# Attention and gated MLP in float32: VectorE block transposes and v products in eight 32x64 tiles from the fifth pair on

## The chip, the cores and the metric

The kernel runs on one core of one Trainium2 chip. The metric is the device time of one execution in microseconds. A core has TensorE (PE, with its weight loads listed apart as PEld), VectorE (DVE), ScalarE (ACT), GpSimd (POOL), SyncE (SP, which issues the DMAs here) and 16 DMA engines.

## The reference

Batch 8, 8 heads, 576 positions, head width 64, model width 512, all float32. Rotary attention is followed by an MLP with a spatial gate:

```python
q_rot, k_rot = (rotate(q), rotate(k))
scores = scale * np.matmul(q_rot, k_rot.transpose(0, 1, 3, 2))
scores = scores - np.max(scores, axis=-1, keepdims=True)
attn = np.exp(scores)
attn = attn / (np.sum(attn, axis=-1, keepdims=True) + 1e-09)
x = np.matmul(attn, v)                       # heads joined to 512 columns
...
h = np.maximum(x @ w_in, 0.0)
u, v = (h[..., :d_ff // 2], h[..., d_ff // 2:])
v_n = (v - mu) / np.sqrt(var + 1e-06)
v_s = np.einsum('ts,bsd->btd', w_spatial, v_n) + b_spatial[None, :, None]
out = (u * v_s) @ w_out
```

## The kernel before

**Pairs.** Two heads of one batch make a pair: 32 pairs, four to a batch. A pair has nine score tiles of 128 queries by 576 keys: four of head 0, four of head 1, and one that holds the last 64 queries of both heads. For each tile TensorE computes scores (`sc`, L542), VectorE the negated row maximum (`nmx`, L563), ScalarE the exponentials with their row sums (`e`, L565). Exact products of float32 are made of a hi part (rounded to the fp32r format by ScalarE) and a lo part (the rest): `qs` and `ks` hold, stacked over 128 partitions, hi and lo of q against hi of k, and `lk` with `qz` (q of one head, zeros for the other) adds hi of q times lo of k.

**Turning and multiplying.** The v product needs the exponentials with keys on the partitions. In the 28 pairs from the fifth on, `values` (L567) does so in three chunks of three tiles: for each of five key blocks, TensorE turns three 128x128 blocks into PSUM (`tp`, L582), ScalarE takes the hi part out (`eh`, L593), VectorE the lo part (`el`, L312), and TensorE multiplies both with v's hi and lo parts (`vs`) into `pv` (L606). Of `pv`, rows 0 to 63 and 64 to 127 are two partial sums; ScalarE copies one (`avt`, L623) and VectorE adds (`x`, L621). The first four pairs (`PLAIN`) use `values_plain` (L626): the same transposes, plain copies out, and float32 products without a split (L679). A float32 product shows as two records in the trace, a product of fp32r as one.

**Preparing a pair.** `prepare` (L381) loads q and k with their swapped halves (`st`), v (`vr`), applies the rotary table on GpSimd (`tabs` for k, `tabq`, a table already scaled by 1/8, for q), splits, and stacks by ten copying DMAs (`qs`, `ks`, `qz`). v's parts are made on ScalarE and GpSimd (L442, L443).

**MLP.** Per batch, `mlp` runs in four stages of matmuls, `pa`, `pb`, `pc` and `pd` (L750, L773, L791, L806), spread between the attention work of the next batch; the last batch's MLP stands alone at the end.

**Order.** Each operation is recorded with a key (its due time, 20 to a pair), costs by engine, and the buffers that it takes. `Program.run` plays the list through with those costs and emits, on each engine, the ready operation with the lowest key whose buffers are free. So the order on each engine is fixed in the program. `SLOTS` says how many buffers a pool has: PSUM has two score buffers of two banks (`sc`), one bank `pv` and three banks `pm` (for `tp` and the MLP).

Of the kernel before, what the change touches and what calls it, by code (L numbers as in the profile page):

```python
# [16 lines left out]
P = 128  # L17
S = 576
# [12 lines left out]
LATENCY = {PE: 200, ACT: 142, DVE: 118, POOL: 95, DMA: 1700}  # L31
TO_PE = 105
LATE = 1500
SLOTS = {
    "stage": 2, "lk": 1, "vraw": 2, "vs": 2, "e2": 4, "e1": 2, "eh": 7, "rb": 1, "x32": 1, "xg": 7, "m": 4,
    "small": 3, "nmx": 3, "rt": 2, "sc": 2, "pv": 1, "pm": 3,
}
PSUM = {"sc": 1024, "pv": 512, "pm": 512}
# [6 lines left out]
CHUNKS = [  # L45
# [54 lines left out]
class Op:  # L100
    def __init__(self, costs, key, f, new, port):
        self.costs, self.key, self.f, self.new, self.port = costs, key, f, new, port
        self.eng, self.late = None, 0
        self.waits, self.after, self.bufs = 0, [], []


class Program:
# [30 lines left out]
    def run(self, make):  # L138
# [22 lines left out]

        busy = dict.fromkeys(LATENCY, False)
# [5 lines left out]
        while events:  # L168
# [23 lines left out]
            for e in LATENCY:  # L192
# [3 lines left out]
                while ready[e] and not chosen:  # L196
                    item = heapq.heappop(ready[e])
                    if item[2].eng:
                        continue
                    other = {DVE: POOL, POOL: DVE}.get(e)  # L200
                    if item[2].port and other and held[other]:
                        passed.append(item)
                    elif place(item[2].new):
                        chosen = item[2]
                    else:
                        passed.append(item)
                for item in passed:
                    heapq.heappush(ready[e], item)
# [15 lines left out]
def tile_attention_gated_mlp(  # L224
# [47 lines left out]
    tabq = T([P, 2 * S], F32, "tabq")  # L272
    ident = T([P, P], F32, "ident")
# [10 lines left out]
    ks = [T([P, TW + S], F32R, f"ks{a}") for a in range(2)]  # L284
    qz = T([P, 2 * S], F32R, "qz")
# [4 lines left out]
    def setup():  # L290
# [5 lines left out]
        fill(qz[64:P, :S], 0.0)  # L296
        fill(qz[0:64, S:], 0.0)
# [19 lines left out]
    def decode(key, where, at, src):  # L317
# [29 lines left out]
        op(DMA, 1500, key - 8, fetch, w=[t0, t1])  # L347
# [9 lines left out]
    def spatial(key, j):  # L357
        st = Buf("xg", [P, 2, S], F32, f"ws{j}")
        op(DMA, 1700, key - 8, lambda: load(st.tile, w_spT[j * P:(j + 2) * P, :].rearrange("(c p) t -> p c t", p=P)), w=[st], new=[st])
# [20 lines left out]

    def prepare(i):  # L381
# [4 lines left out]
        st = [Buf("stage", [P, 2 * S + TW], F32, f"st{i}_{j}") for j in range(2)]  # L386
        lk = Buf("lk", [P, TW + S], F32R, f"lk{i}")
        vr = Buf("vraw", [P, NQ, 2, D], F32, f"vr{i}")
        vs = Buf("vs", [P, NQ, 2, 2, D], F32R, f"vs{i}")
        prepped.append((lk, vr if i < PLAIN else vs))  # L390

        def hi(j, rows=slice(0, P)):

            return st[j][rows, S:2 * S + TW * j].bitcast(F32R)

        def lo_q(e):
            rest_lo(e, st[0][:, :S].bitcast(F32R), st[0][:, :S], hi(0))
# [19 lines left out]
        op(ACT, 573, key - K_HIQ, lambda: round_hi(hi(0), st[0][:, :S]), r=[(st[0], 0)], w=[(st[0], 1)])  # L417
        pair_op(S, key - K_LOQ, lo_q, r=[(st[0], 1)], w=[(st[0], 0)])

        def hi_k():  # L420
            round_hi(hi(1)[:, TW:], st[1][:, :S])
            round_hi(hi(1)[:, :TW], st[1][:, 4 * P:S])

        def lo_k(e):
            rest_lo(e, lk[:, TW:], st[1][:, :S], hi(1)[:, TW:])
            rest_lo(e, lk[:, :TW], st[1][:, 4 * P:S], hi(1)[:, :TW])

        op(ACT, 720, key - K_HIQ, hi_k, r=[(st[1], 0)], w=[(st[1], 1)])
        pair_op(S + TW, key - K_LOK, lo_k, pieces=2, r=[(st[1], 0), (st[1], 1)], w=[lk], new=[lk])
        for a in range(2):  # L430
# [3 lines left out]
            zd = qz[:, a * S:a * S + S]  # L434
            for dst, rows, j, part, tok in (
                (qd, own, 0, 1, ("qs", a, 0)), (kd, own, 1, 1, ("ks", a, 0)), (kd, oth, 1, 1, ("ks", a, 1)),
                (zd, own, 0, 1, ("qz", a)), (qd, oth, 0, 0, ("qs", a, 1)),
            ):
                op(DMA, 650, key - (K_STACK2 if a else K_STACK), lambda dst=dst, rows=rows, j=j, part=part, own=own: load(dst[rows, :].bitcast(F32), hi(j, own).bitcast(F32) if part else st[j][own, :S]), r=[(st[j], part)], w=[tok])
        if i < PLAIN:  # L440
            return
        op(ACT, 627, key + K_V, lambda: round_hi(vs[:, :, :, 0, :], vr.tile), r=[vr], w=[(vs, 0)], new=[vs])  # L442
        pair_op(2 * NQ * D, key + K_VLO, lambda e: e.tensor_tensor(out=vs[:, :, :, 1, :], in0=vr.tile, in1=vs[:, :, :, 0, :].bitcast(F32), op=ALU.subtract), r=[vr, (vs, 0)], w=[(vs, 1)])  # L443

    def prepare_whole(i, b, hp, key):

        q, k = (Buf("xg", [P, 2 * S], F32, f"st{i}_{j}") for j in range(2))
        kf = Buf("xg", [P, TW + S], F32, f"kf{i}")
        vr = Buf("vraw", [P, NQ, 2, D], F32, f"vr{i}")
        prepped.append(((q, kf), vr))  # L450
# [5 lines left out]
        def sum_k(e):  # L456
            e.tensor_tensor(out=kf[:, TW:], in0=k[:, :S], in1=k[:, S:], op=ALU.add)
            e.tensor_tensor(out=kf[:, :TW], in0=k[:, 4 * P:S], in1=k[:, S + 4 * P:], op=ALU.add)

        if i == 0:  # L460
# [4 lines left out]
            op(ACT, 1053, -50, lambda: nc.scalar.activation(tabq, tabs, AF.Copy, scale=0.125), r=["tabs"], w=["tabq"])  # L465
# [13 lines left out]
        else:
            for j, st in enumerate((q, k)):  # L480
                t = ("tabq", "tabs")[j]
                op(DMA, 1640, key - K_LOAD, lambda j=j, st=st: load(st.tile, qk[b, hp, j].rearrange("p c n -> p (c n)")), w=[(st, 0), (st, 1)], new=[st])
                for part in range(2):
                    pair_op(S, key - K_ROPE, lambda e, st=st, part=part, t=(tabq, tabs)[j]: e.tensor_tensor(out=turn(st, part, slice(0, S)), in0=turn(st, part, slice(0, S)), in1=turn(t, part, slice(0, S)), op=ALU.mult), r=[t], w=[(st, part)])
            pair_op(S, key - K_SUM, lambda e: e.tensor_tensor(out=q[:, :S], in0=q[:, :S], in1=q[:, S:], op=ALU.add), r=[(q, 1)], w=[(q, 0)])
            pair_op(S + TW, key - K_SUM, sum_k, pieces=2, r=[(k, 0), (k, 1)], w=[kf], new=[kf])
        op(DMA, 910, key - K_LOAD + 1, lambda: load(vr.tile, v[b, hp]), w=[vr], new=[vr])


    def attention(i):  # L490
        b, hp = pairs[i]
        lk, vs = prepped[i]
        sm = sums[i % 2]
        x32 = Buf("x32", [P, S], F32, f"x32_{i}")
        todo = []
        for c, (tiles, spans) in enumerate(CHUNKS):
            key = 20 * i + 20 / 3 * c
            e2 = Buf("e2", [P, 2 * S], F32, f"e2_{i}_{c}")
            e1 = Buf("e1", [P, S], F32, f"e1_{i}_{c}")
            for n, (a, t) in enumerate(tiles):  # L500
                scores(i, a, t, lk, sm, key + S_AT[n], e1 if n == 2 else e2, n)
            todo.append((key + K_T, c, spans, e2, e1))
        todo.sort(key=lambda x: x[0])
        for n, (key, c, spans, e2, e1) in enumerate(todo):
            values(i, c, spans, e2, e1, vs, x32, key, None if n == 0 else todo[0][1])
# [443 lines left out]
```

## Time and profile before

| | us |
|---|---|
| median of 3 runs | 966.54 (965.38 to 966.99) |
| span of the profiled execution, first to last instruction | 963.6 |
| DMA, mean over the span | 129 GB/s |

The profiled execution has no time of its own on record beside its span; the median of the runs lies 2.9 us above it. In the profile, busy time is the union of an engine's records. Records of TensorE overlap, since the array is pipelined; how long a product holds the queue is read from one start to the next. The DMA engines' busy share in 40 slices of the span, and what they moved:

```profile
DMA  7775634455354554346444444445524455430101
GB/s 273 240 233 170 191 106 124 130 125 140 103 136 127 159 141 114 102 116 171 124 135 118 117 149 122 127 122 152 149 74 132 123 167 144 110 83 13 62 1 50
```

### The profile page before, as it was taken

Reading aid. Unit: us, or ns where it says so; the run is one execution under the profiler, and the core shown is the slowest. Engines: PE = TensorE matmul, PEld = TensorE weight load, DVE = VectorE, ACT = ScalarE, POOL = GpSimd, SP = SyncE. Lnnn points to the kernel's source line nnn. Section 1 sums busy time; section 2 is a strip of 40 time slices with the busy share of each in tenths; the row PEclk is TensorE's granted clock in tenths of the full one; section 3 lists DMA queues with packets and bytes.
Section 4 is the critical chain, followed back from the end, with each engine's and each line's share of the span. In section 5 each row is a group of like instructions: output and inputs, shape, how many; then the busy total and the mean of one; then the engine's idle time right before and its main releaser. Section 6 shows DMA issues by size and latency. Waiting matters only on the chain.

```text
span 963.6 us, 19472 instructions
## 1 busy us (share of the span) xinstructions
PE 934.0 (97%) x6614; PEld 856.2 (89%) x6614; DVE 656.6 (68%) x1461; ACT 738.2 (77%) x1835; POOL 601.1 (62%) x526
## 2 busy tenths in 40 slices
PE   4988899999999999999999999999999999999998
PEld 2555589999899989999899998999889998999998
DVE  5898686766867677665776658676676766866331
ACT  4887788777987779777897779877798678976452
POOL 6775766576758557774765766666586765672121
PEclk9998999999999999999999999999999999999999
DMA  7775634455354554346444444445524455430101
GB/s 273 240 233 170 191 106 124 130 125 140 103 136 127 159 141 114 102 116 171 124 135 118 117 149 122 127 122 152 149 74 132 123 167 144 110 83 13 62 1 50
DMA packets 56037, 124.64 MB, mean 129 GB/s; under 512 B 13185, under 2 KB 13441, under 8 KB 55938
## 3 DMA queue, kind: packets, MB, share of 16 engines
q1 hardware_dynamic: 55938, 123.40, 46.0%
q8 instruction: 53, 0.87, 0.4%
q14 instruction: 46, 0.38, 0.1%
HBM read 66.03 MB, written 9.58 MB: 78 GB/s over the span
## 4 chain that ended last, share of the span: by engine, by line
PE 75%; ACT 13%; DVE 6%; issue 2%; DMA 2%; POOL 1%; SPq 0%; ACTq 0%; DVEq 0%; POOLq 0%
PE sc L542 13%; PE pc L791 12%; PE pv L606 11%; PE tp L582 11%; PE pd L806 10%; PE pb L773 9%; PE pa L750 5%; ACT e L565 4%; ACT eh L593 2%; DVE nmx L563 2%; ACT vv L837 2%; PE pv L679 1%; PE sc L552 1%; DVE el L312 1%; ACT st L309 1%
## 5 line engine op out<-in xcount | busy, mean ns | idle before, releaser
L593 ACT ACTIVATE eh<-tp 128x384 fp32r<-128x384 f32 (+1 forms) x504 | 217.9, 434 | 85.4 <-PE tp L582 68.2
L312 DVE TENSOR_TENSOR el<-tp,eh 128x384 fp32r<-128x384 f32 x336 | 185.9, 554 | 101.9 <-ACT eh L593 88.0
L563 DVE TENSOR_REDUCE nmx<-sc 128x1 f32<-128x576 f32 x288 | 214.9, 749 | 47.9 <-PE sc L542 40.7
L565 ACT ACTIVATE e<-sc,nmx 128x576 f32<-128x576 f32 x288 | 213.2, 741 | 40.1 <-DVE nmx L563 36.0
L582 PE MATMUL tp<-ident,e 128*128 128x128 f32 (+1 forms) x1176 | 195.6, 273 | 1.3 <-DVE eh L312 0.4
L401 POOL TENSOR_TENSOR st<-st,tabq 128x576 f32<-128x576 f32 x62 | 87.9, 1435 | 134.0 <-DMA st<-in_qk_dram 104.5
L582 PEld LDWEIGHTS tp<-ident,e 128*128 128x128 f32 (+1 forms) x1176 | 145.8, 138 | 16.3 <-issue 3.0
L606 PE MATMUL pv<-eh,vs 128*128 128x384 f32 (+1 forms) x560 | 154.5, 317 | 1.5 <-ACT x L685 1.4
L791 PE MATMUL pc<-wsp,vn 128*128 128x288 f32 x768 | 143.1, 303 | 0.0
L773 PE MATMUL pb<-x,wi 128*128 128x288 f32 x768 | 141.8, 306 | 0.6 <-ACT u L776 0.5
L806 PE MATMUL pd<-g,wo 128*128 128x288 f32 x768 | 141.3, 303 | 0.0
L542 PE MATMUL sc<-ks,qs 128*128 128x288 f32 x620 | 133.1, 304 | 4.8 <-ACT e L565 4.3
L750 PE MATMUL pa<-wi,x 128*128 128x512 f32 x448 | 133.2, 407 | 0.0
L542 PE MATMUL sc<-lk,qz 128*128 128x288 f32 x558 | 120.4, 297 | 0.0
L806 PEld LDWEIGHTS pd<-g,wo 128*128 128x128 f32 x768 | 114.0, 189 | 3.4 <-DVE el L312 0.4
L791 PEld LDWEIGHTS pc<-wsp,vn 128*128 128x128 f32 x768 | 114.6, 189 | 1.8
L773 PEld LDWEIGHTS pb<-x,wi 128*128 128x128 f32 x768 | 112.1, 189 | 4.4 <-PE pb L773 1.1
L542 PEld LDWEIGHTS sc<-ks,qs 128*128 128x128 f32 x620 | 100.8, 190 | 15.9 <-ACT e L565 7.2
L606 PE MATMUL pv<-el,vs 128*64 128x384 f32 (+1 forms) x448 | 113.9, 295 | 0.1
L606 PEld LDWEIGHTS pv<-eh,vs 128*128 128x128 f32 x560 | 97.7, 188 | 7.8 <-DVE x L621 2.0
L716 POOL TENSOR_TENSOR x<-x,rb 128x576 f32<-128x576 f32 x32 | 45.9, 1435 | 79.2 <-DVE x L621 73.1
L312 DVE TENSOR_TENSOR eh<-tp,eh 64x256 fp32r<-64x256 f32 (+1 forms) x168 | 59.8, 356 | 51.8 <-ACT eh L593 28.2
(166 smaller groups left out, 1540.6 us busy)
## 6 DMA issues: line engine op xcount, KB each, us to landing
st<-in_qk_dram SPq DMA_DIRECT2D x64, 576.0 KB
ks<-st SPq DMA_DIRECT2D x124, 160.0 KB
qs<-st SPq DMA_DIRECT2D x124, 144.0 KB
vr<-in_v_dram SPq DMA_DIRECT2D x32, 320.0 KB
qz<-st SPq DMA_DIRECT2D x62, 144.0 KB
out_dram<-ob SPq DMA_DIRECT2D x31, 288.0 KB
ws<-in_w_spT_dram SPq DMA_DIRECT2D x2, 576.0 KB
tabs<-in_tab_dram SPq DMA_DIRECT2D x1, 576.0 KB
```

The costliest lines, as they stand in the source:

```text
L312: eng.tensor_tensor(out=lo, in0=src, in1=hi.bitcast(F32), op=ALU.subtract)
L401: f = lambda e: e.tensor_tensor(out=st[j][:, cols], in0=st[j][:, cols], in1=(tabs if j else tabq)[:, cols], op=ALU.mult)
L542: nc.tensor.matmul(pt[:, c * 512:c * 512 + HALF], lhsT=lhsT, rhs=rhs[:, k0 + c * HALF:k0 + (c + 1) * HALF], start=(n == 0), stop=(n == len ...
L563: op(DVE, 665, key + K_MAX, lambda: nc.vector.tensor_reduce(out=nmx.tile, in_=tops(), op=ALU.max, axis=AX.XY, negate=True), r=[pt], w=[nmx ...
L565: op(ACT, 730, key + K_EXP, lambda: nc.scalar.activation(e[:, e0:e0 + S].rearrange("p (c n) -> p c n", c=2), tops(), AF.Exp, bias=nmx.tile ...
L582: nc.tensor.transpose(out=tp[:e.shape[1], m * P:m * P + P], in_=e, identity=ident)
L593: nc.scalar.activation(h, p, AF.Copy)
L606: nc.tensor.matmul(pv[0:rows, c1:c2], lhsT=vs[:, kt, h, vp, :], rhs=part[:, c1:c2], start=(kt == 0 and n == 0 and c1 == 0), stop=last)
L750: nc.tensor.matmul(pm.tile, lhsT=lhsT, rhs=win[1, d][:, j, :], start=(d == 0 and n == 0), stop=(d == 3 and n == len(todo) - 1))
L773: nc.tensor.matmul(pm[:, :HALF], lhsT=win[0, d][:, i, f * P:(f + 1) * P], rhs=x[d][:, at:at + HALF], start=(d == 0 and n == 0), stop=(d == ...
L791: nc.tensor.matmul(pm[:, :HALF], lhsT=lhsT, rhs=rhs, start=(t == 0 and n == 0), stop=(t == 4 and n == 1))
L806: nc.tensor.matmul(pm[:, :HALF], lhsT=wout[d,][:, i, m * P:(m + 1) * P], rhs=gs[d][:, at:at + HALF], start=(d == 0 and n == 0), stop=(d == ...
```

## The change

From the fifth pair on, TensorE's transposes, the hi and lo parts of the exponentials and the split of v are gone. Each exponentials tile is a slice of one buffer `et` (nine tiles of 576, two such buffers), and VectorE transposes it in place in blocks of 32 by 32 (`turn`). Partition group g (32 partitions) then holds, for key block b, 32 keys of each tile's query group g. So v is loaded four times, once into each group of 32 partitions (`vrep`), and TensorE multiplies in float32: 18 key blocks, in each eight products of 32 rows by 64 columns of weights (four groups, two heads) with 160 or 128 columns moving. The eight write four PSUM banks, one for each group: two of a score buffer (`lower`) and two of `pm`. The 18 blocks are two operations of nine blocks, 72 products each; other work may stand between them. The first is placed only when all its banks are free: `reserve` keeps later operations from taking buffers of that pool meanwhile. ScalarE copies the banks of the lower groups out, VectorE those of the upper.

Also: the table `tabq` is gone (1/8 goes into q's split: hi with a scale on ScalarE, lo as a `scalar_tensor_tensor`, now always on VectorE); `qz` is gone, lo of k is stacked per head against zeros (`lks`), so the same q weights serve both score products, and `qt` holds the tail tile's q. The pools change (`pv` is gone, `pm` has four banks), the first four pairs keep TensorE's transposes, with tail blocks by matmuls with the identity, and some planner costs and keys are new.

```diff
 SLOTS = {
-    "stage": 2, "lk": 1, "vraw": 2, "vs": 2, "e2": 4, "e1": 2, "eh": 7, "rb": 1, "x32": 1, "xg": 7, "m": 4,
-    "small": 3, "nmx": 3, "rt": 2, "sc": 2, "pv": 1, "pm": 3,
+    "stage": 3, "lk": 1, "vrep": 1, "et": 2, "rb": 1, "x32": 1, "xg": 7, "m": 4,
+    "small": 3, "nmx": 3, "rt": 2, "sc": 2, "pm": 4, "eh": 6,
 }
...
+        def fetch():
+            rows = v[b, hp].rearrange("(q j) k h d -> j q (k h d)", q=4)
+            for g in range(4):
+                load(vr[32 * g:32 * g + 32].rearrange("j q k h d -> j q (k h d)"), rows)
...
-        pair_op(S, key - K_LOQ, lo_q, r=[(st[0], 1)], w=[(st[0], 0)])
+        op(ACT, 350, key - K_TAIL, tails, r=[(st[0], 1)], w=["qt"])
+        op(DVE, dve_ns(S), key - K_LOQ, lambda: lo_q(nc.vector), r=[(st[0], 1)], w=[(st[0], 0)], port=True)
...
-                parts = [(qs[a][:, a * P + c0:a * P + c0 + P], ks[a]), (qz[:, a * (S + TW) + c0:a * (S + TW) + c0 + P], lk.tile)]
+                q = qs[a][:, a * P + c0:a * P + c0 + P]
+                parts = [(q, ks[a]), (q, lks[a])]
...
+        if turn:
+            op(DVE, 740, key + K_TURN, lambda: nc.vector.transpose(out=et[:, at, :], in_=et[:, at, :]), w=[(et, at)])
...
+        def multiply(b0, b1):
+            parts = [(0, 0, 0, 5, 32), (1, 0, 0, 5, 32), (2, 1, 4, 9, 0), (3, 1, 4, 9, 0), (2, 0, 0, 4, 32), (3, 0, 0, 4, 32), (0, 1, 5, 9, 32), (1, 1, 5, 9, 32)]
+            for b in range(b0, b1):
+                for g, h, s0, s1, c0 in parts:
+                    rows = slice(32 * g, 32 * g + 32)
+                    nc.tensor.matmul(bank(g)[64 * h:64 * h + 64, c0:c0 + 32 * (s1 - s0)], lhsT=vr[rows, b % 4, b // 4, h, :], rhs=et[rows, s0:s1, 32 * b:32 * b + 32], start=(b == 0), stop=(b == NB - 1))
...
+        o = op(PE, 2800, key + K_AV, lambda: multiply(0, half), r=need, w=pv, new=pv)
+        o.reserve, o.late = True, FETCH
+        op(PE, 2800, key + K_AV, lambda: multiply(half, NB), r=need, w=pv)
...
+        def copy_upper():
+            dst = x32[:, :4 * P].rearrange("p (t g i) -> p g t i", t=4, g=4)
+            for g in (2, 3):
+                nc.vector.tensor_copy(out=dst[:, g], in_=bank(g)[:, 32:160].rearrange("p (t i) -> p t i", i=32))
+                nc.vector.tensor_copy(out=x32[64:P, 4 * P + 32 * g - 64:4 * P + 32 * g - 32], in_=bank(g)[64:P, 0:32])
```

On TensorE, before, in the steady part (attention beside `pb` of the MLP), a few rows; `tp_2_4` is the transpose of the last key block of the third chunk, `eh` and `el` are hi and lo of the turned exponentials:

```order
L606 MATMUL pv_2_7262<-eh_2_1_7205,vs_6517 128x384
L606 MATMUL pv_2_7262<-el_2_1_7213,vs_6517 64x384
L773 MATMUL pb_31_7277<-x_5229,wi_605 128x288 x3
L582 MATMUL tp_2_4_7281<-ident,e_17_2_7021 128x128
L582 MATMUL tp_2_4_7281<-ident,e_17_2_7110 64x128
L773 MATMUL pb_31_7277<-x_5691,wi_796 128x288 x3
L582 MATMUL tp_0_0_7291<-ident,e_18_0_7160 128x128 x2
L582 MATMUL tp_0_0_7291<-ident,e_18_0_7211 128x128
```

The same engine now, at the end of a first burst and the start of the second; `pvl` is the lower groups' buffer, `pvu_0` and `pvu_1` are the upper groups' banks:

```order
L603 MATMUL pvl_7272<-et_6786,vr_7047 64x128 x2
L641 MATMUL sc_0_2_7355<-ks_76,qs_74 128x288 x2
L641 MATMUL sc_0_2_7355<-lks_78,qs_74 128x288 x2
L769 MATMUL pc_21_7246<-wsp,vn 128x288 x3
L769 MATMUL pc_30_7369<-wsp,vn 128x288 x3
L769 MATMUL pc_21_7246<-wt_69,vt_72 128x288
L769 MATMUL pc_21_7246<-wt_70,vt_73 128x288
L769 MATMUL pc_30_7369<-wsp,vn 128x288 x6
L769 MATMUL pc_31_7385<-wsp,vn 128x288 x3
L603 MATMUL pvl_7272<-et_6786,vr_7047 64x160 x2
L603 MATMUL pvu_0_7273<-et_6786,vr_7047 64x160
L603 MATMUL pvu_1_7274<-et_6786,vr_7047 64x160
```

Before, v products and transposes stood in threes and twos among the MLP's products; now a pair's v products stand in two blocks of 72, with one score tile and 17 products of the MLP between them here, and no transposes are left on TensorE.

On VectorE, the rows beside the same pair's scores, before:

```order
L312 TENSOR_TENSOR el_0_3_6983<-tp_0_3_6952,eh_0_3_6966 128x384
L829 BN_AGGR sm_4_6972<-sm_4_6972 64x2
L563 TENSOR_REDUCE nmx_1_2_6991<-sc_1_2_6959 128x1
L830 TENSOR_SCALAR sm_4_6972<-sm_4_6972 64x1
L312 TENSOR_TENSOR eh_0_4_6987<-tp_0_4_6977,eh_0_4_6987 64x2x128
L312 TENSOR_TENSOR eh_0_4_6987<-tp_0_4_6977,eh_0_4_6987 64x128
L312 TENSOR_TENSOR el_1_0_7015<-tp_1_0_6997,eh_1_0_7008 128x384
```

And now, with the copies out of the upper groups' banks (L620, L621) and the transposes in place (L665):

```order
L661 TENSOR_REDUCE nmx_0_2_6940<-sc_0_2_6929 128x1
L323 TENSOR_TENSOR vt_72<-vv_4_6718,vt_72 64x512
L665 STREAM_TRANSPOSE et_6786<-et_6786 128x576
L661 TENSOR_REDUCE nmx_0_3_7055<-sc_0_3_7039 128x1
L620 COPY x_17_7044<-pvu_0_6834 128x4x32
L621 COPY x_17_7044<-pvu_0_6834 64x32
L620 COPY x_17_7044<-pvu_1_6835 128x4x32
L621 COPY x_17_7044<-pvu_1_6835 64x32
L661 TENSOR_REDUCE nmx_0_4_7079<-sc_0_4_7063 128x1
L665 STREAM_TRANSPOSE et_6786<-et_6786 128x576 x2
```

The lo parts, which waited for TensorE and ScalarE, have become transposes, which wait for ScalarE's exponentials alone; the copies of the pair before stand among them.

More of the change, by code (lines that the diff above doesn't have):

```diff
@@ L202, in run @@
                         passed.append(item)
+                    elif waiting and item[2] is not waiting[0] and any(b.pools[0] == c.pools[0] for b in item[2].new for c in waiting[0].new):
+                        passed.append(item)
                     elif place(item[2].new):
                         chosen = item[2]
+                        if waiting and chosen is waiting[0]:
+                            waiting.clear()
                     else:
                         passed.append(item)
+                        if item[2].reserve and not waiting:
+                            waiting.append(item[2])
                 for item in passed:
@@ L358, in spatial @@
         st = Buf("xg", [P, 2, S], F32, f"ws{j}")
-        op(DMA, 1700, key - 8, lambda: load(st.tile, w_spT[j * P:(j + 2) * P, :].rearrange("(c p) t -> p c t", p=P)), w=[st], new=[st])
+        op(DMA, dma_ns(576), key - 8, lambda: load(st.tile, w_spT[j * P:(j + 2) * P, :].rearrange("(c p) t -> p c t", p=P)), w=[st], new=[st])
         for c in range(2):
@@ L433, in prepare, with copy @@
             qd, kd = qs[a][:, a * TW:a * TW + S], ks[a]
[L434 to L437, printed above, removed]
-            ):
[L439 to L443, printed above, removed]
+            for dst, rows, part, tok, dep in (
+                (qd, own, 1, ("qs", a, 0), (st[0], 1)), (kd, own, 1, ("ks", a, 0), (st[1], 1)), (kd, oth, 1, ("ks", a, 1), (st[1], 1)),
+                (lks[a], own, 0, ("lks", a), lk), (qd, oth, 0, ("qs", a, 1), (st[0], 0)),
+            ):
+                def copy(dst=dst, rows=rows, own=own, part=part, src=dep[0] if dep is not lk else lk):
+                    load(dst[rows, :].bitcast(F32), src[own, S * part:S * part + S].bitcast(F32))
+                op(DMA, dma_ns(144), key - (K_STACK2 if a else K_STACK), copy, r=[dep], w=[tok])
     def prepare_whole(i, b, hp, key):
         q, k = (Buf("xg", [P, 2 * S], F32, f"st{i}_{j}") for j in range(2))
-        kf = Buf("xg", [P, TW + S], F32, f"kf{i}")
-        vr = Buf("vraw", [P, NQ, 2, D], F32, f"vr{i}")
-        prepped.append(((q, kf), vr))
+        vr = values_tile(i)
+        prepped.append(((q, k), vr))
         c2 = lambda t: t.rearrange("p (c n) -> p c n", c=2)
@@ L474, in turn_q @@
                 nc.vector.tensor_tensor(out=turn(q, 0, cols), in0=turn(q, 0, cols), in1=turn(q, 1, cols), op=ALU.add)
-            op(DVE, 2280, -60, turn_k, r=["tabs"], w=[(k, 0), (k, 1), kf], new=[kf], port=True)
+            op(DVE, 2280, -60, turn_k, r=["tabs"], w=[(k, 0), (k, 1)], port=True)
             for n, (c0, c1) in enumerate(((0, Q0), (Q0, S))):
                 op(DVE, dve_ns(2 * (c1 - c0)) + dve_ns(c1 - c0), -58 + 2 * n, lambda c0=c0, c1=c1: turn_q(slice(c0, c1)), r=[q, "tabs"], w=[(q, n)], port=True)
[L479 to L492, printed above, removed]
+        load_values(vr, b, hp, key)
+    def attention_plain(i):
+        qk_low, vr = prepped[i]
         sm = sums[i % 2]
         x32 = Buf("x32", [P, S], F32, f"x32_{i}")
[L495 to L499, printed above, removed]
-            for n, (a, t) in enumerate(tiles):
[L501 to L505, printed above, removed]
-        normalise(i, sm, x32, 20 * i)
@@ L525, in attention_plain, with bank @@
-        normalise(i, sm, x32, 20 * i)
-    def scores(i, a, t, lk, sm, key, e, n_e):
+        et = Buf("et", [P, 9, S], F32, f"et{i}")
+        for n, (a, t) in enumerate(TILES):
+            scores(i, a, t, qk_low, sm, et, key + S_STEP * n, [et] if n == 0 else [])
+        lower = Buf("sc", None, None, f"pvl{i}")
+        upper = [Buf("pm", None, None, f"pvu{i}_{g}") for g in range(2)]
+        pv = [lower, *upper]
+        def bank(g):
+            return lower[:, 512 * g:512 * g + 512] if g < 2 else upper[g - 2].tile
@@ new lines, in attention, with copy_lower @@
+        need = [vr, *[(et, n) for n in range(9)]]
+        half = NB // 2
+        o = op(PE, 2800, key + K_AV, lambda: multiply(0, half), r=need, w=pv, new=pv)
+        o.reserve, o.late = True, FETCH
+        op(PE, 2800, key + K_AV, lambda: multiply(half, NB), r=need, w=pv)
+        def copy_lower():
+            two = lower.tile.rearrange("p (g n) -> p g n", g=2)
+            dst = x32[:, :4 * P].rearrange("p (t g i) -> p g t i", t=4, g=4)
+            nc.scalar.activation(dst[:, 0:2], two[:, :, 32:160].rearrange("p g (t i) -> p g t i", i=32), AF.Copy)
+            nc.scalar.activation(x32[0:64, 4 * P:].rearrange("p (g i) -> p g i", g=2), two[0:64, :, 160:192], AF.Copy)
@@ L529, in scores @@
+        normalise(i, sm, x32, key)
+    def scores(i, a, t, lk, sm, et, key, new, turn=True):
         pt = Buf("sc", None, None, f"sc{i}_{a}_{t}")
         nmx = Buf("nmx", [P, 1], F32, f"nmx{i}_{a}_{t}")
-        k0 = TW * (n_e != 1)
-        e0 = S * (n_e == 1)
         def mm():
@@ L563, in scores @@
-        op(DVE, 665, key + K_MAX, lambda: nc.vector.tensor_reduce(out=nmx.tile, in_=tops(), op=ALU.max, axis=AX.XY, negate=True), r=[pt], w=[nmx], new=[nmx])
+            q, kw = lk
+            need = [(kw, 0), (kw, 1), (q, 0) if t == 0 else (q, 1), *([(q, 0)] if t else [])]
+        op(PE, 8 * pe_ns(HALF) if i < WHOLE else 4 * pe_ns(HALF) if t < 4 else 6 * pe_ns(HALF), key, mm_whole if i < WHOLE else mm, r=[*need, *([] if new else [(et, "first")])], w=[pt, *([(et, "first")] if new else [])], new=[pt, *new])
@@ L689, in normalise @@
+        op(ACT, 880, key + K_EXP, lambda: nc.scalar.activation(et[:, at, :].rearrange("p (c n) -> p c n", c=2), tops(), AF.Exp, bias=nmx.tile, scale=1.0, accum_out=sm[:, at:at + 1]), r=[pt, nmx], w=[(et, at), ("sums", i % 2, at)])
+        if turn:
+            op(DVE, 740, key + K_TURN, lambda: nc.vector.transpose(out=et[:, at, :], in_=et[:, at, :]), w=[(et, at)])
     def normalise(i, sm, x32, key):
@@ L712, in normalise @@
         op(DVE, 125, key + K_INV, lambda: nc.vector.transpose(out=rt.tile, in_=sm), r=need, w=[rt], new=[rt])
-        op(DMA, 2600, key + K_INV, put, r=[rt], w=[(rt, 1)])
-        op(DMA, 2000, key + K_GET, get, r=[(rt, 1)], w=[rb], new=[rb])
-        whole = [(x32, c) for c in range(len(CHUNKS))]
+        op(DMA, dma_ns(5, 4), key + K_INV, put, r=[rt], w=[(rt, 1)])
+        op(DMA, dma_ns(288, 3), key + K_GET, get, r=[(rt, 1)], w=[rb], new=[rb])
+        whole = [(x32, 0), (x32, 1)]
         pair_op(S, key + K_X, lambda e: e.tensor_tensor(out=x32.tile, in0=x32.tile, in1=rb.tile, op=ALU.mult), r=[rb], w=whole)
@@ L813, in mlp @@
                 continue
-            op(DMA, 800, key + K_OUT, lambda m=m, ob=ob: load(out[b, m * P:(m + 1) * P, :], ob.tile), r=[(ob, 0), (ob, 1)])
+            op(DMA, dma_ns(288), key + K_OUT, lambda m=m, ob=ob: load(out[b, m * P:(m + 1) * P, :], ob.tile), r=[(ob, 0), (ob, 1)])
     def norm(b, t, pm, key, sum_halves):
@@ L858, in tile_attention_gated_mlp @@
     prepped, xs, chain = [], [], []
-    op(POOL, 800, -80, lambda: make_identity(nc, ident), w=["ident"])
-    op(POOL, 800, -26, setup, w=["bias", ("sums", 0, 0), ("sums", 1, 0), ("qz", 0), ("qz", 1), ("qs", 0, 0), ("qs", 1, 0)])
-    for n in range(0):
-        idle = Buf("pv", None, None, f"idle{n}")
-        wide = lambda: ident.rearrange("p (o n) -> p o n", o=1).to_broadcast([P, 4, P])
-        op(PE, 1600, 10000 + n, lambda idle=idle: nc.tensor.matmul(idle.tile.rearrange("p (c n) -> p c n", c=4), lhsT=ident, rhs=wide(), start=True, stop=True), r=["ident"], w=[idle], new=[idle])
+    turns = Buf("vrep", [P, 6 * CW + P], F32, "turns")
+    ident = lambda: turns[:, 6 * CW:]
+    op(POOL, 800, -80, lambda: make_identity(nc, ident()), w=["ident", (turns, 0)], new=[turns])
+    op(POOL, 800, -26, setup, w=["bias", ("sums", 0, 0), ("sums", 1, 0), ("lks", 0), ("lks", 1), "qt", ("qs", 0, 0), ("qs", 1, 0)])
     prepare(0)
```

294 lines of the change are left out of this document (126 added, 168 removed), and 3 rows, old and new, of the table CHUNKS.

## The prediction

> **What bounds the kernel now.** The page's head is read first, then the window view of the steady stretch, because the start looks different.
>
> ```profile
> span 963.6 us, 19472 instructions
> PE 934.0 (97%) x6614; PEld 856.2 (89%) x6614; DVE 656.6 (68%) x1461; ACT 738.2 (77%) x1835; POOL 601.1 (62%) x526
> 120.00:930.00 810.00, 807.74 (x5834) 764.08 (x5833) 557.93 (x1297) 643.27 (x1609) 510.63 (x434) 1.00 0.44 120
> ```
>
> From 120 to 930 us TensorE is busy for 807.74 of 810 us at full clock; VectorE has 558 us, ScalarE 643, GpSimd 511, and the DMA engines are 0.44 busy. TensorE sets the time, so the change is worth what it takes from TensorE's queue. Records of pipelined matmuls overlap, so I count from one start to the next. The chain of waits in one stretch of 40 us (500 to 540) and the line view of the transposes say how much of the queue the changed stage holds:
>
> ```profile
> by line: PE pc L791 35.1%; PE sc L542 18.9%; PE pv L606 18.1%; PE tp L582 16.1%; PE pb L773 12.1%; issue 0.1%
> L582 PE MATMUL tp<-ident,e x1176: 270/272/331, 106.0 to 902.2; 128*128 128x128 f32 x196
> ```
>
> The 28 split pairs (1176 transposes are 28 x 42) run from 106 to 902 us: 796 us, 28.4 us a pair. Transposes (L582) and v products (L606) hold 16.1 + 18.1 = 34.2% of the chain, **9.7 us a pair**. The timeline checks this:
>
> ```profile
> 500.70 0.43 PE L542 MATMUL sc<-ks,qs 128*128 128x288 f32 x2
> 500.97 0.44 PE L542 MATMUL sc<-lk,qz 128*128 128x288 f32 x2
> 501.25 0.49 PE L582 MATMUL tp<-ident,e 128*128 128x128 f32 x3
> 501.49 0.65 PE L773 MATMUL pb<-x,wi 128*128 128x288 f32 x3
> 501.98 0.49 PE L582 MATMUL tp<-ident,e 128*128 128x128 f32 x3
> ...
> 505.37 0.34 PE L606 MATMUL pv<-eh,vs 128*128 128x384 f32 x1
> 505.54 0.34 PE L606 MATMUL pv<-el,vs 128*64 128x384 f32 x1
> 505.72 0.56 PE L773 MATMUL pb<-x,wi 128*128 128x288 f32 x3
> 506.12 0.34 PE L606 MATMUL pv<-eh,vs 128*128 128x384 f32 x1
> ```
>
> Three transposes hold 0.24 us (501.25 to 501.49), and the three products behind them take 0.49 where the same three behind a v product take 0.40 (505.72 to 506.12): 0.33 us a group, and 14 groups' worth (42/3) make 4.6 us a pair. A hi and a lo product of 384 columns hold 0.35 us (505.37 to 505.72); a pair has 15 hi and 12 lo blocks of 384 columns, 13.5 such couples, 4.7 us. Together 9.3; the chain counts what the hand count leaves out (slower steps between unlike forms), so I take 9.65.
>
> **The change, part by part.** *Removed from TensorE:* all of that, 28 x 9.65 = **270 us**. The scores keep their count (38 products a pair) and form.
>
> *Added to TensorE:* 144 f32 products a pair, 32 rows by 64 columns of weights, 160 or 128 columns moving. Such tiles do not occur before; the nearest rows are the f32 products of the first four pairs, where two tiles of 64 columns, or of 64 rows and 64 columns, stand side by side:
>
> ```profile
> 48.43 0.54 PE L679 MATMUL pv<-et_0a,vr 128*64 128x384 f32 x1
> 48.44 0.54 PE L679 MATMUL pv<-et_0b,vr 128*64 128x384 f32 x1
> 48.80 0.49 PE L679 MATMUL pv<-et_0a,vr 128*64 128x384 f32 x1
> 48.81 0.49 PE L679 MATMUL pv<-et_0b,vr 128*64 128x384 f32 x1
> 49.23 0.55 PE L641 MATMUL tp_1b<-ident,e 128*128 128x128 f32 x3
> ...
> 40.07 0.87 PE L679 MATMUL pv<-et,vr 128*64 128x192 f32 x8
> 40.87 0.53 PE L542 MATMUL sc<-ks,qs 128*128 128x288 f32 x2
> ...
> 58.07 0.86 PE L679 MATMUL pv<-et,vr 64*64 64x384 f32 x4
> ```
>
> One f32 product is two records (passes), and two tiles start 0.01 us apart: they run together, also when rows differ (58.07: four records, two products, in 0.86 us). The weight loads of the same products:
>
> ```profile
> 48.43 0.13 PEld L679 LDWEIGHTS pv<-et_0a,vr 128*64 128x64 f32 x1 [0.17 <-issue]
> 48.44 0.13 PEld L679 LDWEIGHTS pv<-et_0b,vr 128*64 128x64 f32 x1
> 48.48 0.14 PEld L679 LDWEIGHTS pv<-et_0a,vr 128*64 128x64 f32 x1
> 48.49 0.14 PEld L679 LDWEIGHTS pv<-et_0b,vr 128*64 128x64 f32 x1
> ...
> 40.07 0.52 PEld L679 LDWEIGHTS pv<-et,vr 128*64 128x64 f32 x8 [0.17 <-ACT x L685]
> ```
>
> A first pass of 384 columns takes 0.37 us (48.43 to 48.80), of which 0.05 is the first load (48.43 to 48.48), so 0.32 us of streaming, 0.83 ns a column. Four passes of 192 columns in each of two tiles then need 0.64, and the stretch takes 0.80 (40.07 to 40.87): entering and leaving such a stage costs 0.16 us. If eight tiles run like two, a block costs two passes of 160 columns, 0.27 us; nine blocks and 0.16 make 2.6 us a burst, 56 bursts **146 us**. The bounds lie far apart: one tile at a time, 288 passes of 0.12 us are 35 us a pair (980 us more); all hidden is 0. I take the row's value, since it has tiles that differ in rows and in columns at once.
>
> Here a rule of the Trainium skill speaks against the change. The page "TensorE: Matmul & The Clock Gate", section "Part 3: Packing small matmuls — row/col tiling", says that a weight load overlaps running matmuls only where the row group differs; two of the eight tiles share each row group, and every tile is reloaded 36 times a pair. By that rule each pass would also pay its load. The trace disagrees: the eight loads at 40.07 share all rows, and the last is over 0.52 us after the first began, while the matmuls run for 0.87.
>
> *Instruction supply.* The page's queue rows:
>
> ```profile
> q1 hardware_dynamic: 55938, 123.40, 46.0%
> q8 instruction: 53, 0.87, 0.4%
> ```
>
> 53 packets for TensorE's 13,228 records (6614 and 6614) are 16 KB and some 250 records each; 0.4% of 16 engines' 963.6 us is 1.16 us a packet. A burst has 72 x 4 = 288 records, so it uses up more than one packet in 2.6 us, where a packet lasts 18 us now. Bounds: 0, or 1.16 us in each of 56 bursts, 65 us. With one packet in reserve only a burst that crosses two borders waits, about one in eight: **8 us**.
>
> *VectorE.* Gone are 12 lo parts a pair and the last blocks, and the adds; new are nine transposes of 128x576, lo of q, and four small copies.
>
> ```profile
> L563 DVE TENSOR_REDUCE nmx<-sc 128x1 f32<-128x576 f32 x288 | 214.9, 749 | 47.9 <-PE sc L542 40.7 <-PE sc L552 4.2 <-PE tp L641 0.6
> L312 DVE TENSOR_TENSOR el<-tp,eh 128x384 fp32r<-128x384 f32 x336 | 185.9, 554 | 101.9 <-ACT eh L593 88.0 <-PE pv L606 3.8 <-PE pb L773 3.2
> L712 DVE STREAM_TRANSPOSE rt<-sums 128x32 f32<-128x32 f32 x32 | 6.5, 204 | 0.4
> ```
>
> A transpose of 32 columns takes 204 ns; 192 columns more cost 195 ns between the other two rows, so 576 columns at that rate are 0.76 us (bounds: 0.20, the row as it stands, and 1.31 at half the rate). Nine are 6.8 us a pair, about what the twelve lo parts were (12 x 0.554 = 6.6). VectorE keeps its 558/810 x 28.4 = 19.6 us a pair, but the pair shrinks to 28.4 - 9.65 + 5.4 = 24.2 us: 81% busy, still beside TensorE. ScalarE loses all hi parts, and GpSimd v's and q's lo: neither comes near.
>
> *DMA.* v comes four times: 28 x 960 KB is 27.5 MB more, ks is 124 x 16 KB (2 MB) less: 149 MB. At 123.4 MB for 46% of 963.6 us this is 535 us of the engines, 62% of the new time. One v tile is loaded between a pair's second burst and the next pair's first, some 24.2 - 8 = 16 us; 1.31 MB need 10 us at the mean 129 GB/s. On SP the stacking copies of the pair after next stand behind that load's wait, and TensorE needs them a pair later: nothing.
>
> *New waits.* During a burst VectorE and ScalarE get no scores; one score buffer and two pm buffers are held for both bursts and the MLP groups between, and matmuls behind the waiting burst, of the MLP and the scores, stand still. TensorE's waits for ScalarE, at the change from plain to split pairs:
>
> ```profile
> 115.06 0.52 PE L542 MATMUL sc<-ks,qs 128*128 128x288 f32 x2 [0.54 <-ACT e L565]
> ...
> 117.84 0.44 PE L606 MATMUL pv<-eh,vs 128*128 128x384 f32 x1 [1.36 <-ACT x L685]
> ```
>
> Bounds 0 and 1.36 us a pair; I take the smaller row, 0.54 x 28 = **15 us**, as MLP work is there to cover. The plain pairs turn their tail blocks by f32 products instead of transposes: ten a pair, two at a time, 128 columns each, a third of 0.80: 1.3 us for about 0.5 before, **3 us** in four pairs (bounds 0 and 5). The table of q is off every queue that waits: 0.
>
> *Sum:* 963.6 - 270 + 146 + 8 + 15 + 3 = 865.6 us of span. The median of the runs, 966.54, is 2.9 above the span; with it **868 us**.
>
> **The rivals.** *Loads not hidden* (the page's rule, as a mechanism of this kernel): every pass waits 0.05 us for its own weights, as the first one does at 48.43; 36 passes a pair, 28 pairs: 50 us, 918. Against it: the loads at 40.07. *Every burst waits for instructions:* 65 us in place of 8: 925. For it: 288 records against 250; against it: no wait of that kind now. *VectorE becomes the bound:* transposes at half rate cost 9 x 0.55 = 5 us a pair, 24.6 against 24.2 us, and in-order waits beside a full engine add about 1 us: 868 + 40 = 908. For it: only a 32-column transpose is in the trace. *The loads of eight tiles queue up on one path* at 0.05 us each (the step of one tile's two loads): 288 are 14.4 us a pair where 5.2 were counted; **slower**, 868 + 28 x 9.2 = 1126. It decides from 0.033 us a pass on (9.65 us over 288 passes). Against it: four loads of two tiles in 0.06 us; for it: never more than two tiles' loads stood side by side. Beside it stands the same page's section "Wait — 56ns, not 53.3ns?", which gives 62 ns a matmul where the sequencer's program decodes each; by it a pair would take 17.9 us (an estimate from that page), and no run here shows so dense a stretch. *The change doesn't shorten the queue,* since the burst's buffers hold up the MLP as long as it saves: about 965.
>
> **How the numbers follow.** Forecast 0.66; instructions 0.10; loads 0.06; VectorE 0.06; loads queued 0.10; no gain 0.02. The forecast itself spans 838 (no new waits, supply free) to 890. The range 838 to 940 takes in the first four. Faster by over 0.2% (about what a measurement of this kernel can tell from no change): 0.88, same 0.02, slower 0.10.
>
> **What would show it.** A burst of 72 products lasting about 2.6 us, its first eight matmuls some 0.01 us apart, is the concurrency; 7 us would be the queue of loads. TensorE waits put down to issue inside bursts are the supply. STREAM_TRANSPOSE near 760 ns, VectorE at about 80% in the steady stretch, TensorE still over 95%. Wrong would be TensorE well under 95% there: then another engine or a buffer sets the pair.

## The result and the profile after

The changed kernel takes 879.81 us (median of 4 runs, 876.26 to 882.97) against 966.52 us before (4 runs, 965.38 to 966.99): ratio 0.911, 95% interval 0.908 to 0.914. The profiled execution took 876.26 us, its span is 874.5. Runs over 1.5% above the fastest of their kernel are left out of ratios. Head of the page after, the window view of the steady stretch, and the queue rows:

```profile
span 874.5 us, 30219 instructions
PE 824.3 (94%) x12554; PEld 744.4 (85%) x12554; DVE 602.2 (69%) x1213; ACT 517.2 (59%) x1303; POOL 512.0 (59%) x433
...
120.00:840.00 720.00, 695.11 (x11687) 647.45 (x11675) 510.93 (x1061) 427.53 (x1087) 426.67 (x351) 1.00 0.68 172
...
q1 hardware_dynamic: 68034, 148.90, 65.8%
q8 instruction: 99, 1.62, 0.8%
```

TensorE is still the fullest engine, 695.11 of 720 us (97%), but where 2 us of 810 were free before, 25 of 720 are now. ScalarE has dropped from 79% to 59% of the steady stretch. One burst in TensorE's timeline (first and last rows; the rows between are the same in kind):

```profile
481.70 0.42 PE L769 MATMUL pc<-wsp,vn 128*128 128x288 f32 x2
482.05 0.35 PE L603 MATMUL pvl<-et,vr 32*64 32x160 f32 x2
482.06 0.35 PE L603 MATMUL pvu<-et,vr 32*64 32x160 f32 x4
482.09 0.44 PE L603 MATMUL pvl<-et,vr 32*64 32x128 f32 x3
...
484.44 0.28 PE L603 MATMUL pvl<-et,vr 32*64 32x128 f32 x2
484.65 0.54 PE L641 MATMUL sc<-ks,qs 128*128 128x288 f32 x2
```

Nine records of eight tiles start within some 0.05 us, and the 72 products are over after 2.60 us (482.05 to 484.65, the start of the product behind them). Read so for all 56 bursts, the median is 2.60 us and the sum 162.7 us: 56 x 2.60 would be 145.6, so 17 us are stalls inside bursts. One of them, and the line view's account of what TensorE (products and loads together) waited for at L603:

```profile
708.96 0.40 PE L603 MATMUL pvl<-et,vr 32*64 32x128 f32 x3
711.05 0.35 PE L603 MATMUL pvl<-et,vr 32*64 32x160 f32 x2 [1.69 <-issue]
...
  issue: 29.2, 62
```

Nothing that the profile shows was awaited in the middle of that burst. But the trace also has every packet of q8, the queue that brings TensorE's instructions: one was on its way from 708.80 to 709.76, and the stall ended 1.29 us after it. Of the 13 gaps of over 0.4 us between starts inside bursts, 11 (12 us of the 17) end 1.1 to 1.7 us after the end of such a packet; a moment picked at random between 120 and 800 us lies so in 8% of cases. The other two are put down to PSUM banks that came free late (ACT `vv` L802, DVE `u` L831). The supply of instructions is tested below.

### The profile page after: what moved, and what is told of

Read it like the earlier page. It is cut to its first block, busy times and chain, and to the rows that moved or that the text cites. A ratio compares the mean times of both kernels' runs of the same rounds, so it can differ in the third digit from the quotient of the medians.

```text
span 874.5 us, 30219 instructions
## 1 busy us (share of the span) xinstructions
PE 824.3 (94%) x12554; PEld 744.4 (85%) x12554; DVE 602.2 (69%) x1213; ACT 517.2 (59%) x1303; POOL 512.0 (59%) x433
## 3 DMA queue, kind: packets, MB, share of 16 engines
q1 hardware_dynamic: 68034, 148.90, 65.8%
## 4 chain that ended last, share of the span: by engine, by line
PE 59%; POOL 12%; DVE 9%; DMA 8%; ACT 7%; issue 3%; SPq 1%; POOLq 0%; ACTq 0%; DVEq 0%
PE sc L641 10%; PE pa L728 9%; PE pvu L603 9%; PE pd L784 8%; PE pc L769 8%; PE pvl L603 6%; DMA qs<-st 5%; PE pb L751 4%; POOL st L433 3%; DVE nmx L661 3%; POOL lk L323 2%; ACT et L663 2%; PE pv L573 2%; POOL st L437 2%; POOL x L323 2%
## 5 line engine op out<-in xcount | busy, mean ns | idle before, releaser
L663 ACT ACTIVATE et<-sc,nmx 128x576 f32<-128x576 f32 x288 | 212.0, 737 | 115.1 <-DVE nmx L661 114.4
L433 POOL TENSOR_TENSOR st<-st,tabs 128x576 f32<-128x576 f32 x124 | 175.4, 1432 | 111.0 <-DMA st<-in_qk_dram 66.2
L665 DVE STREAM_TRANSPOSE et<-et 128x576 f32<-128x576 f32 x252 | 191.5, 766 | 38.0 <-ACT et L663 36.2
L603 PE MATMUL pvl<-et,vr 32*64 32x160 f32 (+1 forms) x4032 | 155.3, 294 | 9.1 <-issue 6.3
L603 PEld LDWEIGHTS pvl<-et,vr 32*64 32x64 f32 x4032 | 137.7, 131 | 22.4 <-issue 16.9
L603 PE MATMUL pvu<-et,vr 32*64 32x128 f32 (+1 forms) x4032 | 152.8, 294 | 3.6 <-issue 2.6
L641 PE MATMUL sc<-ks,qs 128*128 128x288 f32 x620 | 135.1, 307 | 18.1 <-ACT et L663 8.8
L603 PEld LDWEIGHTS pvu<-et,vr 32*64 32x64 f32 x4032 | 122.2, 130 | 5.2 <-issue 3.5
L641 PE MATMUL sc<-lks,qs 128*128 128x288 f32 x496 | 106.2, 296 | 0.0
L728 PEld LDWEIGHTS pa<-wi,x 128*128 128x128 f32 x448 | 81.9, 192 | 16.2 <-issue 1.3
L437 POOL TENSOR_TENSOR st<-st 128x576 f32<-128x576 f32 x62 | 89.2, 1439 | 3.8
```

What stands on the lines that cost most here:

```text
L437: f = lambda e: e.tensor_tensor(out=st[j][:, :S], in0=st[j][:, :S], in1=st[j][:, S:2 * S], op=ALU.add)
L603: nc.tensor.matmul(bank(g)[64 * h:64 * h + 64, c0:c0 + 32 * (s1 - s0)], lhsT=vr[rows, b % 4, b // 4, h, :], rhs=et[rows, s0:s1, 32 * b:32 ...
L641: nc.tensor.matmul(pt[:, c * 512:c * 512 + HALF], lhsT=lhsT, rhs=rhs[:, c * HALF:(c + 1) * HALF], start=(n == 0), stop=(n == len(parts) - 1))
L663: op(ACT, 880, key + K_EXP, lambda: nc.scalar.activation(et[:, at, :].rearrange("p (c n) -> p c n", c=2), tops(), AF.Exp, bias=nmx.tile, s ...
L665: op(DVE, 740, key + K_TURN, lambda: nc.vector.transpose(out=et[:, at, :], in_=et[:, at, :]), w=[(et, at)])
L728: nc.tensor.matmul(pm.tile, lhsT=lhsT, rhs=win[1, d][:, j, :], start=(d == 0 and n == 0), stop=(d == 3 and n == len(todo) - 1))
```

## The experiments

In all of them the planner's order matters: an edit inside an operation leaves the order of every engine as it is, an edit of an operation's cost, key or number gives a new order everywhere, and some us of the difference may come from that alone.

**Four tiles side by side in place of eight** (order unchanged):

```diff
-            for b in range(b0, b1):
-                for g, h, s0, s1, c0 in parts:
+            for head, b in [(head, b) for head in range(2) for b in range(b0, b1)]:
+                for g, h, s0, s1, c0 in [p for p in parts if p[1] == head]:
```

> The same products, but in each burst first the nine blocks of one head and then those of the other, so that four tiles stand side by side in place of eight; the order on every engine is otherwise unchanged. If the eight tiles run together and the weight loads are hidden, a burst grows from 2.6 us to two times 18 passes of 0.133 us and 0.16 us, about 5.0 us, and the time by 56 x 2.4 = 134 us, to about 1014 us. If a burst is set by the number of its loads or by the supply of instructions, its 72 products last 2.6 us as before and the time stays near 880 us.

Measured: 964.46 us (one run). A burst in its timeline:

```profile
210.32 0.35 PE L603 MATMUL pvl<-et,vr 32*64 32x160 f32 x2
210.33 0.43 PE L603 MATMUL pvu<-et,vr 32*64 32x128 f32 x4
...
214.89 0.40 PE L784 MATMUL pd<-g,wo 128*128 128x288 f32 x1
```

The burst lasts 4.57 us. The products, their columns and their loads are the same in number, so none of these counts sets the length by itself: what differs is how many columns pass one after the other, 9 x 2 x 160 for a tile that runs beside the other head's, 9 x 2 x (160 + 128) where the two heads take turns (9 blocks, two passes each). The expected 5.0 was mis-added: each partition group streams 160 columns for one head and 128 for the other, 9 x 2 x 288 x 0.83 ns = 4.3 us and the entry. The sum over 56 bursts is 257.8 us, 95 more than with eight tiles, and the time is 85 us longer. With four tiles the kernel is where it was before the change (966.28 in the same series, one run each): the gain hangs on the eight. And the stalls are gone: 257.8 against 56 x 4.57 = 255.9, and none of the gaps left ends behind a q8 packet. A burst that uses up its records at 57% of the pace doesn't run dry.

**VectorE's transposes, longer and shorter** (order unchanged). Twice, so that a tile ends unturned:

```diff
-lambda: nc.vector.transpose(out=et[:, at, :], in_=et[:, at, :])
+lambda: [nc.vector.transpose(out=et[:, at, :], in_=et[:, at, :]) for n in range(2)]
```

> Each exponentials tile is transposed twice, so it ends unturned and the v products use unturned blocks; the order is unchanged. VectorE gets 9 x 0.766 = 6.9 us more a pair, 26.8 us in place of 19.9, where a pair lasts 25.2 us. If TensorE sets the pair now and VectorE has slack of about 5 us, VectorE becomes the bound and the time grows by 28 x (26.8 - 25.2) = 45 us or somewhat more for waits in order, 925 to 960 us. If VectorE sets the pair already, the time grows by the full 28 x 6.9 = 193 us, to 1073 us.

Measured: 963.89 us (one run). Shorter, with `[:, at, :32]` in both places:

> Each VectorE transpose takes the first 32 of 576 columns only, the rest of a tile stays unturned; the order is unchanged. VectorE loses 9 x 0.56 = 5 us a pair. If TensorE's queue sets the pair, little changes: 865 to 880 us, the waits of TensorE for scores may shrink. If VectorE stands in the way of TensorE, the pair falls towards TensorE's own 24 us, and the time to 845 us or less.

Measured: 880.51 us (4 runs, 877.77 to 882.09), ratio to before 0.910 (0.907 to 0.913). The window view from 200 to 700 us of the changed kernel, of the short and of the double transposes, the last with two rows of its waits view (total, times, longest):

```profile
200.00:700.00 500.00, 485.97 (x8318) 453.43 (x8317) 358.69 (x730) 299.75 (x767) 318.27 (x260) 1.00 0.74 184
```

```profile
200.00:700.00 500.00, 482.72 (x8285) 450.42 (x8285) 268.10 (x723) 297.60 (x761) 314.13 (x256) 1.00 0.73 183
```

```profile
200.00:700.00 500.00, 451.44 (x7345) 409.42 (x7345) 428.59 (x801) 263.08 (x682) 278.37 (x229) 1.00 0.66 165
...
PE sc L641 <- ACT et L663: 46.9, 52, 3.4
...
PE pvl L603 <- ACT et L663: 16.9, 18, 3.5
```

The third column pair is VectorE: 91 us less in 500 change nothing, so VectorE doesn't hold TensorE up. With double transposes VectorE is busy for 86% and TensorE for 90%: neither is full, and yet 84 us of 28 x 6.9 = 193 arrive, where 45 to 80 were expected. The expectation had VectorE's load too high: 358.69 of 500 us are 18.1 us of a 25.2 us pair, not 19.9, and 6.9 more would still fit into the pair. What grows is waiting: TensorE's waits for score buffers go from 8.8 to 46.9 us, those at the start of a burst for ScalarE's exponentials from 2.6 to 16.9 us. So the order of the engines passes VectorE's load on before VectorE is full.

**One burst of 144 products, or four of 40 and 32** (a new order):

```diff
-        o = op(PE, 2800, key + K_AV, lambda: multiply(0, half), r=need, w=pv, new=pv)
-        o.reserve, o.late = True, FETCH
-        op(PE, 2800, key + K_AV, lambda: multiply(half, NB), r=need, w=pv)
+        o = op(PE, 5600, key + K_AV, lambda: multiply(0, NB), r=need, w=pv, new=pv)
+        o.reserve = True
```

> The two bursts of a pair are one operation of 144 products; the planner moves the work that stood between them. If instructions arrive in packets of about 250 records and one is in reserve, 576 records in a row run dry in every pair, so the stalls inside bursts rise from 17 us to 28 x 1.1 to 28 x 2, 31 to 56 us, and the time to 890 to 920 us. If the stalls inside bursts have another cause (a late semaphore), they don't grow with the length of the burst, and the time stays at 875 to 882 us.

Measured: 948.45 us (4 runs, 945.82 to 957.49), ratio 0.983 (0.977 to 0.988). A burst now lasts 8.1 us in the mean, where 18 blocks and one entry need 5.0: 87 us over, more than expected. One of the stalls, the account at L603, and the window view during and after that stall:

```profile
436.81 0.48 PE L603 MATMUL pvu<-et,vr 32*64 32x160 f32 x3 [3.44 <-issue]
...
  issue: 129.6, 86
...
433.00:436.70 3.70, 0.37 (x15) 0.08 (x5) 0.00 (x0) 0.00 (x0) 1.48 (x2) 1.00 0.75 279
436.70:440.10 3.40, 3.29 (x105) 3.11 (x104) 0.00 (x0) 0.00 (x0) 3.32 (x3) 0.50 0.04 14
```

Of the 36 gaps of over 0.4 us, 34 end 1.1 to 1.7 us after a packet of q8, and they make 68 of the 87 us. A second cost hides behind them: the third number from the end is TensorE's granted clock, and after this stall it is 0.50, so that the 6.6 blocks left take about 0.5 us each in place of 0.27. From 120 us on this happens 12 times for 48 us in all (once, for 3.4 us, in the changed kernel); 28 us at half clock lie inside bursts and cost about 14 us there (an estimate: half of them).

The four bursts are written the same way, with blocks 0 to 5, 5 to 9, 9 to 14 and 14 to 18 and half of `FETCH` between:

> Four operations of 40, 32, 40 and 32 products in place of two of 72, with other work between. If the stalls inside bursts are the supply of instructions, they nearly go (17 us to under 5), and two more entries and exits of 0.16 us cost 9 us: 872 to 880 us. If buffers that are held longer cost more than that, 885 to 900 us.

Measured: 915.49 us (4 runs, 910.02 to 920.85), ratio 0.947 (0.942 to 0.952). The bursts sum to 161.6 us where 56 x (1.52 + 1.25) = 155 are due, so stalls inside have fallen to 6.5 us, a little over the expected 5, and only 0.7 us of them lie in a gap behind a q8 packet. But the time is 36 us longer, above both ranges. What TensorE waits for is in the waits view, below.

**The time between the two bursts** (a new order): `FETCH`, 2500 in the changed kernel, set to 0 and to 5000, and three bursts of six blocks with 1200 between.

> The planner is not told to keep the second burst 2.5 us behind the first; it may follow as soon as its key says. If instruction supply needs the time between bursts, stalls inside bursts rise from 17 us towards the 87 us of the single burst, and the time to 890 to 945 us. If the split alone matters, 875 to 885 us.

Measured: 927.11 us (4 runs, 923.63 to 933.37), ratio 0.960 (0.956 to 0.964); the bursts sum to 202.5 us, 57 over what is due: 37 in gaps behind a q8 packet (24 of 25 gaps), and about 12 from half clock.

> The planner keeps the second burst 5 us behind the first in place of 2.5. If the remaining stalls come from a packet still on its way from the burst before, they fall from 17 us to under 8; the score buffer and two pm buffers are held 2.5 us longer in each pair. If held buffers cost TensorE work, as four bursts suggest, the time is 890 to 920 us; if not, 865 to 880 us.

Measured: 920.35 us (4 runs, 918.44 to 926.27), ratio 0.953 (0.949 to 0.957); the bursts sum to 158.5 us, 13 of them stalls, not under 8 (8.0 in gaps behind a q8 packet).

> Three bursts of six blocks (192 records each), 1.2 us planned between them in place of 2.5, so that a pair's buffers are held about as long as now. If the stalls come from bursts that use up more records than a packet holds, they fall from 17 us to about 5, and one more entry of 0.2 us a pair costs 6 us: 868 to 878 us. If the number of interruptions itself is what made four bursts slow, about 895 us.

Measured: 890.01 us (median of three runs, 886.15 to 892.75; a fourth took 901.22), ratio 0.920 (0.916 to 0.925); 84 bursts sum to 160.1 us, 10 of them stalls. A miss: fewer stalls, and yet 10 us more, nearer to the rival's 895.

TensorE's waits for scores, in the waits views of the changed kernel, of 5000 between, and of the four bursts:

```profile
PE sc L641 <- ACT et L663: 8.8, 8, 1.8
PE sc L641 <- DMA qs<-st: 7.3, 8, 1.7
```

```profile
PE sc L641 <- DMA qs<-st: 26.9, 17, 2.4
PE sc L641 <- ACT et L663: 20.7, 22, 1.8
```

```profile
PE sc L641 <- ACT et L663: 23.8, 24, 2.0
PE sc L641 <- DMA qs<-st: 14.2, 10, 2.5
```

A score product that waits for ScalarE's exponentials waits for its PSUM buffer. While a pair's bursts last, one of the two score buffers is theirs; the longer that is, the more often the other one is late. The new order also brings the copies of q in later. Against the changed kernel, these two rows are 31 us more with 5000 between, where the profiled span is 50 us longer; the clock is at half for 38 us there (10 times from 120 us on), which costs about 17 us more than the 3.4 us before (an estimate: half of the difference). With four bursts the two rows are 22 us more, where the span is 42 us longer; shorter stalls and more entries and exits nearly cancel, about 3 us are the clock's, and the rest stays open. So the distance between the bursts has a price on both sides: instructions when it is short, score buffers when it is long, and in both cases a slower clock behind the waits.

**v loaded after the next pair's copies** (a new order): the load's key is `key + 13` in place of `key - K_LOAD + 1`.

> The fourfold load of v has a later key, so the next pair's stacking copies are issued ahead of it. TensorE waits 7 us in all for the copies of q that land 6.5 us after their issue, behind 1.3 MB of v. If v's load is what delays them, these waits go and the time falls by 5 to 8 us, to about 872 us. If v then lands too late for its burst, TensorE waits for v in its place and the time rises by up to 1 us a pair, to 900 us.

Measured: 879.31 us (4 runs, 875.34 to 885.54), ratio 0.910 (0.906 to 0.915): no difference. The waits for q fell from 7.3 to 5.4 us only. Whether v's load delays those copies stays open; they are not worth more than these 7 us.

**Bursts of one block** (order unchanged; most of the v product is left out):

```diff
-            for b in range(b0, b1):
+            for b in (0,) if b0 == 0 else (NB - 1,):
```

> Each burst multiplies one key block of its nine (8 products for 72), so most of the v product is left out; transposes, copies, loads and the order are unchanged. TensorE loses 16 blocks of 0.27 us, 4.3 us a pair, and the 17 us of stalls inside bursts. If the bursts lie on the path with their full length, the time falls by 28 x 4.3 + 17 = 137 us to about 743 us, less what VectorE, busy for 19.9 us of a pair that would then last 20.3, holds back: 743 to 790 us. If the pair is set by buffers that a burst holds or by transfers, it falls by less than 50 us, to over 830 us.

Measured: 830.72 us (one run), at the near edge of the second range: 49 us arrive. The bursts, read to the start of the product behind, sum to 50.0 us, but a burst of one block and its entry needs 0.43, 24 us in all; most of the other 26 are waits of the product behind the burst, a score product in 16 of 17 cases. So some 139 of 162.7 us are freed, as expected, and 35% of that arrives:

```profile
200.00:700.00 500.00, 445.10 (x3376) 398.26 (x3375) 378.86 (x762) 311.67 (x810) 330.82 (x270) 0.97 0.78 195
...
PE sc L641 <- ACT et L663: 58.5, 49, 3.4
```

TensorE waits for score buffers now (58.5 us where it was 8.8), and neither it (89%) nor VectorE (76%) is full. Its clock is at half for 55 us from 120 us on, which costs about 26 us more than before (an estimate, as above). The chain of score, maximum and exponential through its two buffers looks like the next bound, in this order; no run with a third buffer tests it.

Each part of the change was not undone by itself: the stacking of lo of k per head, the missing table of q and `reserve` were left as they are.

## Why the prediction was right, point by point

- *TensorE's queue sets the time:* right. Shorter transposes change nothing, longer bursts (four tiles) arrive with 85 of 95 us. Shorter bursts arrive with 49 of 139 us only, so it sets the time as long as score buffers come in time.
- *Eight tiles run like two, 2.6 us a burst:* right, 2.60 us at the median. The weight loads are hidden, in tiles that share a partition group too: a burst with the loads of every one of its 18 passes exposed by 0.05 us would have been 0.9 us longer. The Trainium skill's rule (page "TensorE: Matmul & The Clock Gate", section "Part 3: Packing small matmuls — row/col tiling") that loads overlap only where row groups differ is not borne out by this burst.
- *Nor does a decoder hold it back:* 144 matmul records in 2.60 us are 18 ns each. The Trainium skill (page "TensorE: Matmul & The Clock Gate", section "Wait — 56ns, not 53.3ns?") has about 62 ns a matmul where the sequencer's program decodes; this burst is not held to that. The slower rival, loads that queue up at 33 ns or more a pass, falls with the 18 ns.
- *What is removed, 9.65 us a pair:* borne out by the pace, though not measured by itself. From 204 to 784 us, 23 pairs start their bursts 25.2 us apart; 28.4 - 9.65 + 5.2, with 0.6 of stalls and some 0.5 of other waits, is 25.05.
- *Supply of instructions, 8 us:* the mechanism was right, the size was off: 17 us of stalls, 12 of them behind a q8 packet. The step that was mis-sized is "one in eight": 11 of 56 bursts have such a gap, one in five, with 1.1 us each. How many packets lie in reserve was assumed, and no run measures it. A single burst (68 us in such gaps) and bursts close together (37 us) show that it is supply over time, not only a border crossed twice. That a stall can bring the clock down behind it was in no term; in the changed kernel it cost about 2 us (an estimate: half of 3.4).
- *VectorE keeps 19.6 us a pair:* mis-sized. A transpose is 766 ns (0.76 was expected), but the last blocks and the adds of the two halves, which go, weigh 4.1 us a pair before, and lo of q and the small copies only 1.9 now; the prediction let them cancel. 510.93 of 720 us are 71%, not 81%. It cost nothing, as VectorE isn't the bound.
- *DMA:* 148.90 MB as counted, 65.8% of the engines where 62 were expected. "Nothing" for the copies behind v's load was near: the waits for q are 7 us, of unsettled cause.
- *New waits, 15 us:* in the steady stretch TensorE is free for 25 us, with most of the stalls in it; 8.8 and 7.3 us before scores fit the term.
- *Sum:* a span of 865.6 was worked out, 874.5 was measured. Stalls of 17 us where 8 were counted are of the size of that difference; the other terms lie close, but may offset one another by some us. The median lies 5.3 us over this span, where 2.9 was added, as the profiled execution is the fastest of the four.

## What to carry to other kernels

Where a contraction can be cut into 32-row pieces, float32 products in eight tiles of 32x64 replace transposes and a hi and lo split: what counts is how many columns pass one after the other, so all tiles have to be fed in turn (four tiles side by side gave the whole gain back). Here such bursts needed instructions faster than they were delivered, so cut them and put other work between; but the PSUM buffers that stay taken meanwhile starve the stage that fills them, and of the distances run the one between was best. Look at the granted clock when TensorE has waits: it can make a wait dearer than its length. Price a burst on the critical engine, then ask what is next: here only 35% of what a shorter burst freed arrived.

## What the runs showed of the hardware

The supply of TensorE's instructions can be a limit: 99 packets of 16 KB came in the changed kernel and 53 in the one before, and a stream of 288 records in 2.6 us (loads and matmuls, 111 a us) ran dry after some 2 to 5 us when it went on without a break, for 0.4 to 4 us at a time (2.4 us behind packets for each burst of 144 products). It went on 1.1 to 1.7 us after the end of a packet that itself took about 1 us. At 63 records a us (four tiles) it did not run dry.

TensorE's granted clock fell to half for 3.4 or 6.8 us at a time. From 120 us to 20 us before the end, all the runs together have 52 such drops (none in the kernel before), and every one begins behind 3.4 us in which TensorE was idle for 1.2 to 3.4 us; half of all such stretches have no idle time at all. Some stretches as idle are not followed by a drop.

A STREAM_TRANSPOSE of 128x576 float32 in place takes 766 ns.
